# Linear attention and a sine layer on one core: the first chunk's loads, transposes and spare products in another order

## The chip, the core and the metric

The kernel runs on one core of a Trainium2 chip. The metric is the device time of one execution in microseconds, the median of several runs. A profile comes from one execution of its own, and its times are counted from the first instruction that the profiler saw (the span).

## What is computed

Linear attention with decay over B=4 sequences, H=8 heads, S=768 positions and D=64, in blocks of 64 positions, and behind it a layer with a sine:

```python
intra = np.einsum('bhic,bhjc->bhij', qb, kb) * Dmask[None]
intra = np.einsum('bhij,bhjd->bhid', intra, vb)
inter = np.einsum('bhid,bhde->bhie', qb * lam_pow[None], kv_state)
out[:, :, sl] = intra + inter
kv_state = lam_block * kv_state + np.einsum('bhsd,bhse->bhde', kb * rev_pow[None], vb)
...
h = x @ w_in                          # 3072 x 512 by 512 x 2048
s = np.sin(alpha * h)
g = h + s * s / (alpha + 1e-09)
return g @ w_out                      # 3072 x 2048 by 2048 x 512
```

`x` is the attention's output with the heads side by side.

## The kernel before, in words

The positions are cut into six chunks of 128 (`t` or `g`, 0 to 5); a chunk holds all four sequences (`b`), so 512 rows. While the layer runs for chunk g, the attention of chunk g+1 is woven in between. The order on every engine is the order of the program; nothing is rearranged by a scheduler. An engine waits only where it reads or reuses what another has not finished.

**Loads.** Two ways lead into the chip. SP's queue brings k and q of sequence 0 and q of sequence 1 of the first chunk as float32 (`raw`, L79 to L81) and then `alpha`. GpSimd's queue brings everything else and turns it to bfloat16 on the way: `load(t, nm, b0, b1)` (L100 to L104), `load_w_in0`, `load_w_in`, `load_w_out` (L88 to L98). For the first chunk its order is: index tables by `iota` (`pcol`, L110 to L117), the identity `iden`, the triangle `tri`, `pos_row`; then k of b=1, k of b=2 and 3, q of b=2 and 3 (L133, L134); then `idf`, both halves of v, five loads of `w_in`, and later two of `w_out`. GpSimd builds the list of packets of each of its loads itself and keeps at most eight loads outstanding: a further one waits for the eighth before it to land. The third and fourth part of `w_out` (L487, L488) stand behind chunk 1's k, q and v in that queue.

**The first chunk's attention** (L443 to L477). Its state is empty, so only the part inside the chunk is computed. ScalarE makes powers of lambda from `pcol` and `pos_row` (`powers`, `decay_tables`, `etab`); DVE casts raw k (L445), scales raw q (`scale_q`, L447) and makes the mask `C0` (L451) from `tri`. Then, per sequence b: TensorE transposes k and q into a bank of PSUM (`turns` for b=0 and 1, L221; `turns_pair` for b=2 and 3, L240, which does k of both sequences, then q of both); ScalarE, for one copy DVE, takes them to `QKT` (L231, L248, L250); `scores1` (L252) multiplies k and q, eight small products of two heads each, and DVE masks them (`STm`, L260); `outs` (L263) multiplies by v, and ScalarE (b=0 and 1, L276) or DVE (b=2 and 3, L278) takes the result to `xt`.

**Spare products.** `spin(n)` (L437) multiplies a tile of ones, `fill`, n times into a bank; nothing reads the result. It stands at the start (10), between the transposes of k and q of b=2 and 3 (6) and at the end (2).

**Order on the engines around the change.** TensorE: transposes b=0, b=1; scores b=0, b=1; the transpose of `alpha` (L461); k's late transposes (bank 1); six spare products; q's late transposes (bank 2, both sequences); scores b=2, b=3; outputs b=0 to 3; two spare products; the hidden layer. DVE: the copy of q's b=3, `alpha_sb` (L467) and its reciprocal (L468), four masks, two `xt`. ScalarE: the copies, the casts of outputs b=0 and 1, then the table for the sine and a warm-up of one element (L473, L474).

**The layer.** `hidden(g, f)` (L382) makes 128 of the 2048 hidden columns: four products (L386), the sine on ScalarE (L389), its square on ScalarE or DVE. `finish` (L397) puts the result into `gall` on DVE (L401). `project(g, m, part)` (L406) multiplies four of the sixteen blocks of `gall` by one of the four parts of `w_out` (L411); for chunk 0 the third parts come right behind the late transposes of chunk 1 (L537 to L545).

Of the kernel before, what the change touches and what calls it, by code (L numbers as in the profile page):

```python
# [9 lines left out]
ACTF = mybir.ActivationFunctionType  # L10
FP32 = mybir.dt.float32
BF16 = mybir.dt.bfloat16
# [3 lines left out]
def kernel(  # L16
# [11 lines left out]
    nc = tc.nc  # L28
    P = nc.NUM_PARTITIONS
# [4 lines left out]
    HP = H // 2  # L34
# [8 lines left out]
    consts = ctx.enter_context(tc.tile_pool(name="consts", bufs=1))  # L43
# [14 lines left out]
    def bank(nm, n, dtype=FP32):  # L58
        return psum.tile([P, 512 if dtype is FP32 else 1024], dtype, name=nm, tag=f"b{n}")

    HB = (0, 1, 2)
# [34 lines left out]
    def load_w_out(i):  # L96
        nc.gpsimd.dma_start(out=w_out_sb[i][:],
                            in_=moe_w_out[i * 512:(i + 1) * 512, :].rearrange("(f p) d -> p f d", p=P))  # L98

    def load(t, nm, b0, b1):  # L100
        dst, src = NAT[nm]
        nc.gpsimd.dma_start(  # L102
            out=dst[t][:, b0:b1, :, :].rearrange("p b h e -> p (b h) e"),
            in_=src[b0:b1, :, t * T:(t + 1) * T, :].rearrange("b h p e -> p (b h) e"))  # L104
# [2 lines left out]
    new_chunk(1)  # L107


    pcol = consts.tile([P, 5], FP32, name="pcol")  # L110
    for n, base, step in ((0, -1, -1), (1, 1, 1), (2, T - 1, -1)):
        nc.gpsimd.iota(out=pcol[:, n:n + 1], pattern=[[0, 1]], base=base, channel_multiplier=step,
# [5 lines left out]
    iden = consts.tile([P, P], BF16, name="iden")  # L118
# [7 lines left out]
    for n in (1, 2, 0):  # L126
# [3 lines left out]
    pos_row = consts.tile([P, T], FP32, name="pos_row")  # L130
    nc.gpsimd.iota(out=pos_row[:], pattern=[[1, T]], base=1, channel_multiplier=0,
                   allow_small_or_imprecise_dtypes=True)
    for nm, b0, b1 in (("k", 1, 2), ("k", 2, 4), ("q", 2, 4)):  # L133
        load(0, nm, b0, b1)  # L134
    idf = consts.tile([NFC, NFC], FP32, name="idf")
    make_identity(nc, idf[:])
    for nm, b0, b1 in (("v", 0, 2), ("v", 2, 4)):
# [6 lines left out]
    lnlam = consts.tile([P, H], FP32, name="lnlam")  # L144
# [41 lines left out]
    V, G, A = nc.vector, nc.gpsimd, nc.scalar  # L186
    xt = {}
    kdec = {}
    KT, QT, both = {}, {}, {}
    STm = {}  # L190
    def home(t, blk):
        return SBD[2 if blk else t % 2]
# [44 lines left out]
    def halves(hd):  # L237
        return slice(hd * D, (hd + 1) * D)

    def turns_pair(t, nm, b, bk, engines):  # L240
        ps = bank("T_ps", bk, BF16)[:].rearrange("p (u c i) -> p u c i", u=2, c=HP)
        src, n = (kn, 0) if nm == "k" else (qn, 1)
        for u in range(2):
            for hp in range(HP):
                nc.tensor.transpose(out=ps[:, u, hp, :], in_=src[t][:, b + u, 2 * hp:2 * hp + 2, :], identity=iden[:])
        for u, eng in enumerate(engines):
            if eng is nc.scalar:
                eng.copy(out=both[t][:, n, b + u, :, :], in_=ps[:, u])  # L248
            else:
                eng.tensor_copy(out=both[t][:, n, b + u, :, :], in_=ps[:, u])  # L250

    def scores1(t, b, ns):  # L252
        Fb = [bank("F0_ps", n)[:].rearrange("p (c i) -> p c i", c=HP) for n in ns]
        for hp in range(HP):
            for hd in range(2):
                nc.tensor.matmul(out=Fb[hd][:, hp, :], lhsT=KT[t][halves(hd), b, hp, :],  # L256
                                 rhs=QT[t][halves(hd), b, hp, :], start=True, stop=True)
        st = work.tile([P, 2, HP, T], BF16, name="STm")
        for hd in range(2):
            nc.vector.tensor_tensor(out=st[:, hd], in0=Fb[hd], in1=C0[:, hd], op=ALU.mult)  # L260
        STm[t, b] = st

    def outs(t, b, n, eng=None):  # L263
        O = bank("O_ps", n)[:].rearrange("p (c i) -> p c i", c=HP)
        if t:
            for hp in range(HP):
                nc.tensor.matmul(out=O[:, hp, :], lhsT=home(t, 0)[:, b, hp, :, :], rhs=QT[t][:, b, hp, :],
                                 start=(hp == 0), stop=False, skip_group_check=True)
        for hp in range(HP):
            for hd in range(2):  # L270
                nc.tensor.matmul(out=O[halves(hd), hp, :], lhsT=vn[t][:, b, 2 * hp + hd, :],
                                 rhs=STm[t, b][:, hd, hp, :], start=(t == 0 and hp == 0), stop=True,
                                 skip_group_check=True)
        x = xt[t][:, :, b * T:(b + 1) * T]
        if eng is nc.scalar:
            nc.scalar.copy(out=x, in_=O)  # L276
        else:
            nc.vector.tensor_tensor(out=x, in0=O, in1=Etab[:], op=ALU.mult)  # L278
# [155 lines left out]
            row = m * S + g * T  # L434
            nc.sync.dma_start(out=out[row:row + T, cols], in_=o_sb[:, 0:DM // 2])

    def spin(n, cols=512):  # L437
        ps = bank("hps", HB[0])
        for _ in range(n):
            nc.tensor.matmul(out=ps[:, 0:cols], lhsT=fill[:, 0:P], rhs=fill[:, 0:cols], start=True, stop=True)  # L440


    new_xt(0)  # L443
    spin(10)
    nc.vector.tensor_copy(out=kn[0][:, 0, :, :], in_=raw["k", 0][:])  # L445
    def scale_q(b):
# [14 lines left out]
    nc.tensor.transpose(out=a_ps[:, 0:NFC], in_=alpha_fp[:], identity=idf[:])  # L461
    alpha_sb = consts.tile([P, NFC], FP32, name="alpha_sb")
    r_sb = consts.tile([P, NFC], FP32, name="r_sb")
    turns_pair(0, "k", 2, 1, (A, A))
    spin(6)
    turns_pair(0, "q", 2, 2, (A, V))
    nc.vector.tensor_copy(out=alpha_sb[:], in_=a_ps[:, 0:NFC])  # L467
    nc.vector.reciprocal(out=r_sb[:], in_=alpha_sb[:])  # L468
    scores1(0, 2, (6, 7))
    scores1(0, 3, (4, 5))  # L470
    outs(0, 0, 0, A)
    outs(0, 1, 3, A)
    warm = consts.tile([P, 1], FP32, name="warm")  # L473
    nc.scalar.activation(out=warm[:], in_=lnlam[:, 0:1], func=ACTF.Sin)  # L474
    outs(0, 2, 1)
    outs(0, 3, 2)
    spin(2)  # L477
    load_w_out(0)
    load_w_out(1)
    decay_k(0, 0, 2)  # L480
# [156 lines left out]
```

## Time and profile before

| | us |
|---|---|
| three runs | 215.69, 217.07, 215.86 |
| median | 215.86 |
| the profiled execution | 215.78 |
| its span | 214.1 |
| TensorE matmul, busy in the span | 200.0 (93%) |
| ScalarE, busy | 140.6 (66%) |
| VectorE (DVE), busy | 139.0 (65%) |
| GpSimd (POOL), busy | 96.4 (45%) |
| GpSimd's load queue: 75968 packets, 13.24 MB | 84.5% of 16 engines' span |
| SP's load queue: 23648 packets, 11.28 MB | 26.9% of 16 engines' span |
| GpSimd: index tables, identity, triangle | 0.91 to 2.72 |
| GpSimd: issues of k b=1, then k b=2 and 3 | 2.66 to 4.88 |
| first product of the hidden layer | 20.40 |

Reading it: "busy" counts instructions of an engine from start to end; matmuls overlap each other, so 93% is not the array at its peak. A packet is one contiguous run of bytes. The views used are the page (its rows of tenths over 40 slices), the chain of waits (followed back from the last instruction: start, length, what ran), timelines of an engine, windows (length, then busy time and number of instructions of PE, weight loads, DVE, ACT and POOL, the granted clock, the transfer engines' share and GB/s), and the list of transfers with the time from issue to landing.

### The profile page before, as it was taken

What the parts mean: (1) busy time and instruction counts of PE and PEld (TensorE: products, weight loads), DVE (VectorE), ACT (ScalarE), POOL (GpSimd) and SP (SyncE); (2) the same over time, 40 slices, a digit from 0 to 9 for tenths busy, and PEclk for the clock granted to TensorE, in tenths of its full rate; (3) what the DMA queues carried; (4) which work ended last, traced back from release to release, by engine and by line L of the source; (5) the groups of instructions that cost most, each with busy time, mean ns of one, the idle gap of its engine ahead of it and who ended that gap; (6) DMA issues with size and microseconds to landing.
All of it is one profiled execution on the core that took longest, in us unless ns stands there. A gap on an engine that the chain in (4) does not pass through costs nothing.

```text
span 214.1 us, 4756 instructions
## 1 busy us (share of the span) xinstructions
PE 200.0 (93%) x1913; PEld 100.5 (47%) x1939; DVE 139.0 (65%) x251; ACT 140.6 (66%) x225; POOL 96.4 (45%) x111
## 2 busy tenths in 40 slices
PE   7486989999998999999999999999999999999993
PEld 2354444554444644446444456444446444444453
DVE  7637697865899966995757977648668544444000
ACT  5834997736766497667576765776765778888121
POOL 8999639795699995899001950003100000000000
PEclk9769999999999999999999999999999999999999
DMA  5999999999999999999999114911101001110212
GB/s 113 163 164 206 206 181 156 182 176 158 199 159 161 165 134 129 210 174 115 166 134 163 73 52 104 144 49 52 43 9 49 26 26 49 49 48 5 100 49 98
DMA packets 99782, 24.83 MB, mean 116 GB/s; under 512 B 91936, under 2 KB 96816, under 8 KB 99760
## 3 DMA queue, kind: packets, MB, share of 16 engines
q0 software_dynamic: 75968, 13.24, 84.5%
q1 hardware_dynamic: 23648, 11.28, 26.9%
q8 instruction: 15, 0.25, 0.5%
q14 instruction: 7, 0.06, 0.1%
q10 hardware_dynamic: 144, 0.00, 0.0%
HBM read 27.28 MB, written 6.29 MB: 157 GB/s over the span
## 4 chain that ended last, share of the span: by engine, by line
PE 78%; DVE 10%; ACT 5%; DMA 3%; issue 2%; POOL 1%; POOLq 0%; ACTq 0%
PE ops L411 35%; PE hps L386 32%; DVE gall L401 3%; DMA kn<-in_k_dram 3%; ACT s_sb L389 2%; DVE STm L260 2%; DVE S L297 2%; PE O_ps L352 2%; PE hps L429 2%; ACT s L392 2%; PE O_ps L360 1%; PE T_ps L227 1%; DVE s L400 1%; PE hps L440 1%; PE F_ps L256 1%
## 5 line engine op out<-in xcount | busy, mean ns | idle before, releaser
L401 DVE SCALAR_TENSOR_TENSOR gall<-s,r_sb,hps 128x512 bf16<-128x512 bf16 x96 | 70.9, 744 | 42.3 <-ACT s L392 42.0
L386 PE MATMUL hps<-xt,w_in 128*128 128x512 bf16 x377 | 95.6, 379 | 2.6 <-DVE gall L401 1.5
L389 ACT ACTIVATE s_sb<-hps,alpha_sb 128x512 bf16<-128x512 f32 x96 | 65.6, 687 | 42.7 <-PE hps L386 42.3
L411 PE MATMUL ops<-w_out,gall 128*128 128x512 bf16 x351 | 90.7, 379 | 0.9 <-issue 0.3
L386 PEld LDWEIGHTS <-w_in 128*128 128x128 bf16 x384 | 37.3, 98 | 46.6 <-issue 2.3
L392 ACT ACTIVATE s<-s_sb 128x512 bf16<-128x512 bf16 x87 | 54.9, 632 | 2.8
L411 PEld LDWEIGHTS <-gall 128*128 128x128 bf16 x368 | 34.6, 98 | 40.3 <-issue 0.6
L301 POOL CAST sbd<-S 64x512 bf16<-64x512 f32 x36 | 22.4, 623 | 45.4 <-DVE S L297 43.9
L204 POOL TENSOR_TENSOR kdec<-kn,R 128x1024 bf16<-128x1024 bf16 x12 | 22.6, 1901 | 0.4
L297 DVE SCALAR_TENSOR_TENSOR S<-S,L,KV_ps 128x128 f32<-128x128 f32 x64 | 17.3, 342 | 0.0
L102 POOL DMA_DIRECT2D vn<-in_v_dram x12 | 14.0, 1168 | 1.4 <-DMA w_in<-in_moe_w_in_dram 1.4
L420 ACT COPY o_sb<-ops 128x512 f32<-128x512 f32 x11 | 6.3, 577 | 12.2 <-PE ops L411 12.2
L102 POOL DMA_DIRECT2D kn<-in_k_dram x12 | 14.1, 1173 | 0.5 <-DMA kn<-in_k_dram 0.5
L102 POOL DMA_DIRECT2D qn<-in_q_dram x11 | 13.0, 1180 | 1.7 <-DMA qn<-in_q_dram 1.0
L260 DVE TENSOR_TENSOR STm<-F_ps,C 128x512 bf16<-128x512 f32 x16 | 10.1, 682 | 3.8 <-PE F_ps L256 3.7
L368 DVE TENSOR_TENSOR xt<-O_ps,Etab 128x512 bf16<-128x512 f32 x16 | 10.3, 685 | 2.5 <-PE O_ps L360 2.5
L418 DVE COPY o_sb<-ops 128x512 f32<-128x512 f32 x12 | 8.3, 692 | 4.9 <-PE ops L411 4.9
L341 DVE TENSOR_TENSOR STm<-F_ps,C 128x512 bf16<-128x512 f32 x16 | 10.3, 683 | 0.0
L440 PE MATMUL hps<-fill 128*128 128x512 bf16 x16 | 6.5, 565 | 1.7 <-DVE fill L121 1.5
L235 ACT COPY QKT<-T_ps 128x1024 bf16<-128x1024 bf16 x4 | 3.9, 1008 | 2.2 <-PE T_ps L227 2.2
L256 PE MATMUL F_ps<-QKT 64*128 64x128 bf16 x64 | 3.6, 239 | 1.7 <-ACT QKT L248 0.7
L400 DVE TENSOR_TENSOR s<-s_sb 128x512 bf16<-128x512 bf16 x9 | 5.1, 571 | 0.0
(71 smaller groups left out, 97.6 us busy)
## 6 DMA issues: line engine op xcount, KB each, us to landing
out_dram<-o_sb SPq DMA_DIRECT2D x23, 256.0 KB, 2.3
vn<-in_v_dram POOLq DMA_DIRECT2D x12, 256.0 KB, 15.1
kn<-in_k_dram POOLq DMA_DIRECT2D x11, 256.0 KB, 12.0
qn<-in_q_dram POOLq DMA_DIRECT2D x11, 256.0 KB, 14.0
w_out<-in_moe_w_out_dram POOLq DMA_DIRECT2D x4, 512.0 KB, 15.6
w_in<-in_moe_w_in_dram POOLq DMA_DIRECT2D x3, 512.0 KB, 12.2
raw_q<-in_q_dram SPq DMA_DIRECT2D x2, 256.0 KB, 5.2
w_in<-in_moe_w_in_dram POOLq DMA_DIRECT2D x2, 256.0 KB, 7.3
```

The lines of the kernel that those rows point to most:

```text
L102: nc.gpsimd.dma_start(out=dst[t][:, b0:b1, :, :].rearrange("p b h e -> p (b h) e"), in_=src[b0:b1, :, t * T:(t + 1) * T, :].rearrange("b h ...
L204: nc.gpsimd.tensor_tensor(out=kdec[t][:, b0:b1, :, :], in0=kn[t][:, b0:b1, :, :], in1=R[:].unsqueeze(1).unsqueeze(3).broadcast_to([P, b1 - ...
L260: nc.vector.tensor_tensor(out=st[:, hd], in0=Fb[hd], in1=C0[:, hd], op=ALU.mult)
L297: nc.vector.scalar_tensor_tensor(out=S[:, bs, hp, :], in0=old[:, bs, hp, :], scalar=decay[:, hp:hp + 1], in1=ps[:, :, hp, :], op0=ALU.mult ...
L301: nc.gpsimd.tensor_copy(out=dst[halves(hd), bs, :, hd, :], in_=S[halves(hd), bs, :, :])
L341: nc.vector.tensor_tensor(out=st[:, hd], in0=att["F"][pr, hd], in1=C64[:, hd].unsqueeze(1).broadcast_to([P, 2, HP, D]), op=ALU.mult)
L368: nc.vector.tensor_tensor(out=xview(t)[:, 2 * pr:2 * pr + 2, blk, :, :], in0=att["O"][pr, blk], in1=Eb, op=ALU.mult)
L386: nc.tensor.matmul(out=hps[:], lhsT=w[:, c, (f % 4) * P:(f % 4 + 1) * P], rhs=xt[g][:, c, :], start=(c == 0), stop=(c == NDC - 1))
L389: nc.scalar.activation(out=s_sb[:], in_=hps[:], func=ACTF.Sin, scale=alpha_sb[:, f:f + 1])
L392: nc.scalar.activation(out=s2[:], in_=s_sb[:], func=ACTF.Square)
L401: nc.vector.scalar_tensor_tensor(out=gall[g][:, f, :], in0=s2[:], scalar=r_sb[:, f:f + 1], in1=hps[:], op0=ALU.mult, op1=ALU.add)
L411: nc.tensor.matmul(out=ops[:], lhsT=gall[g][:, f, m * P:(m + 1) * P], rhs=w_out_sb[part][:, f % 4, :], start=(f == 0), stop=(f == NFC - 1))
```

## The change

Four things, all in the first chunk. GpSimd issues both loads of k ahead of its index tables, q's stays behind them. `turns_pair` takes two banks, one for each sequence; q's late transposes use banks 2 and 0, k's both bank 1 as before. The six spare products ahead of q's transposes are gone; instead one stands behind them, two behind the scores, two each behind the outputs of b=1 and b=2, and three instead of two at the end, each call in a bank that it names. On ScalarE the sine's table and the warm-up come ahead of the casts of outputs b=0 and 1; on DVE `alpha_sb` and the reciprocal come between the masks of b=2 and b=3.

```diff
     new_chunk(1)
+    load(0, "k", 1, 2)
+    load(0, "k", 2, 4)
     pcol = consts.tile([P, 5], FP32, name="pcol")
...
-    for nm, b0, b1 in (("k", 1, 2), ("k", 2, 4), ("q", 2, 4)):
-        load(0, nm, b0, b1)
+    load(0, "q", 2, 4)
     idf = consts.tile([NFC, NFC], FP32, name="idf")
...
     def turns_pair(t, nm, b, bk, engines):
-        ps = bank("T_ps", bk, BF16)[:].rearrange("p (u c i) -> p u c i", u=2, c=HP)
         src, n = (kn, 0) if nm == "k" else (qn, 1)
+        one = bank("T_ps", bk[0], BF16)[:].rearrange("p (u c i) -> p u c i", u=2, c=HP)
+        two = one if bk[0] == bk[1] else bank("T_ps", bk[1], BF16)[:].rearrange("p (u c i) -> p u c i", u=2, c=HP)
+        ps = (one[:, 0], two[:, 1])
...
-    def spin(n, cols=512):
-        ps = bank("hps", HB[0])
+    def spin(n, bk=0, cols=512):
+        ps = bank("hps", bk)
...
-    turns_pair(0, "k", 2, 1, (A, A))
-    spin(6)
-    turns_pair(0, "q", 2, 2, (A, V))
+    turns_pair(0, "k", 2, (1, 1), (A, A))
+    turns_pair(0, "q", 2, (2, 0), (A, V))
+    warm = consts.tile([P, 1], FP32, name="warm")
+    nc.scalar.activation(out=warm[:], in_=lnlam[:, 0:1], func=ACTF.Sin)
+    spin(1, 1)
+    scores1(0, 2, (6, 7))
     nc.vector.tensor_copy(out=alpha_sb[:], in_=a_ps[:, 0:NFC])
     nc.vector.reciprocal(out=r_sb[:], in_=alpha_sb[:])
-    scores1(0, 2, (6, 7))
     scores1(0, 3, (4, 5))
+    spin(2, 1)
     outs(0, 0, 0, A)
     outs(0, 1, 3, A)
-    warm = consts.tile([P, 1], FP32, name="warm")
-    nc.scalar.activation(out=warm[:], in_=lnlam[:, 0:1], func=ACTF.Sin)
+    spin(2, 1)
     outs(0, 2, 1)
+    spin(2, 2)
     outs(0, 3, 2)
-    spin(2)
+    spin(3, 4)
     load_w_out(0)
```

More of the change, by code (lines that the diff above doesn't have):

```diff
@@ L240, in turns_pair @@
     def turns_pair(t, nm, b, bk, engines):
-        ps = bank("T_ps", bk, BF16)[:].rearrange("p (u c i) -> p u c i", u=2, c=HP)
         src, n = (kn, 0) if nm == "k" else (qn, 1)
+        one = bank("T_ps", bk[0], BF16)[:].rearrange("p (u c i) -> p u c i", u=2, c=HP)
+        two = one if bk[0] == bk[1] else bank("T_ps", bk[1], BF16)[:].rearrange("p (u c i) -> p u c i", u=2, c=HP)
+        ps = (one[:, 0], two[:, 1])
         for u in range(2):
             for hp in range(HP):
-                nc.tensor.transpose(out=ps[:, u, hp, :], in_=src[t][:, b + u, 2 * hp:2 * hp + 2, :], identity=iden[:])
+                nc.tensor.transpose(out=ps[u][:, hp, :], in_=src[t][:, b + u, 2 * hp:2 * hp + 2, :], identity=iden[:])
         for u, eng in enumerate(engines):
             if eng is nc.scalar:
-                eng.copy(out=both[t][:, n, b + u, :, :], in_=ps[:, u])
+                eng.copy(out=both[t][:, n, b + u, :, :], in_=ps[u])
             else:
-                eng.tensor_copy(out=both[t][:, n, b + u, :, :], in_=ps[:, u])
+                eng.tensor_copy(out=both[t][:, n, b + u, :, :], in_=ps[u])
     def scores1(t, b, ns):
```

## The prediction

> **What bounds the kernel now.** I read the clock and transfer rows of the profile's second part first, then the chain of waits over the first 48 us, then the windows of the clock, the queues' packets and the transfers' landing times.
>
> ```profile
> PEclk9769999999999999999999999999999999999999
> DMA  5999999999999999999999114911101001110212
> ```
>
> Each digit is 5.35 us. The clock is low only in the first three slices. The transfer engines are 90% busy from the second slice to the 22nd, so whatever lands there lands when the queue gets to it.
>
> ```profile
> 2.66 5.59 DMA kn<-in_k_dram
> 8.29 1.05 PE T_ps L227 x8
> ...
> 12.50 2.33 PE hps L440 x5
> 14.83 0.46 PE T_ps L245 x8
> 15.29 0.02 issue
> 15.31 0.60 ACT QKT L248
> 15.91 0.02 issue
> 15.93 0.42 DVE QKT L250
> ...
> 16.72 2.33 DVE STm L260 x4
> 19.06 0.51 DVE xt L278
> 19.57 0.01 issue
> 19.57 0.69 DVE xt L278
> 20.26 0.14 issue
> 20.40 1.04 PE hps L386 x4
> ```
>
> The first chunk is one chain: k's load, the spare products (L440) between the transposes of k and q, two copies one after the other, four masks on DVE, the outputs to `xt`, and at 20.40 the first product of the hidden layer. From there PE is nearly always busy.
>
> ```profile
> 8.00:11.30 3.30, 2.39 (x26) 1.74 (x27) 2.03 (x5) 1.86 (x4) 3.30 (x5) 0.50 2.46 156
> 11.30:14.70 3.40, 3.18 (x15) 1.75 (x16) 1.10 (x2) 1.07 (x2) 3.08 (x5) 0.50 3.25 156
> 14.70:18.10 3.40, 2.29 (x49) 1.79 (x48) 2.13 (x6) 1.49 (x3) 3.39 (x4) 1.00 1.41 199
> ```
>
> After the length comes PE's busy time; the clock is third from the end. The clock fell at 7.9 and rose at 14.7, two steps of 3.4: 72% busy did not lift it, 94% did, and 67% kept it up.
>
> ```profile
> 28.92 0.75 POOL L97 DMA_DIRECT2D w_out<-in_moe_w_out_dram  x1 [1.38 <-DMA w_out<-in_moe_w_out_dram]
> w_out<-in_moe_w_out_dram POOLq DMA_DIRECT2D x1, 512.0 KB, 15.5
> 44.45 1.03 PE L411 MATMUL ops<-w_out,gall 128*128 128x512 bf16 x4
> ```
>
> The third part of `w_out`, issued at 28.92, lands 15.5 later, at 44.42. Its first product starts at 44.45. A front end that is ready earlier meets this load.
>
> **The change, part by part.** Times are those of the profiled execution: 215.78 us, a span of 214.1 and 1.68 around it; the median of the three runs is 215.86, 0.08 more.
>
> *GpSimd's order.* The two k issues took 2.22 us from 2.66; now they start at about 0.81, where SP and ScalarE start theirs. The index work (0.91 to 2.72) ends at about 4.9. Its readers: the exponentials from 5.39 (their columns ready by about 3.9), the transposes at 5.57 (`iden` at 4.5), `pos_row` at 6.56 (4.9), `C0` at 6.81 (`tri` at 4.7). The smallest slack is 1.1 us: nothing is lost, and without that cover at most 2.2 - 1.1 = 1.1 would be. GpSimd's sum up to q's issue is unchanged, so q, `idf`, v, `w_in` and `w_out` are issued as before (q at 4.86).
>
> What it costs lies on SP's queue: the raw loads of k0, q0 and q1 share the engines with k. In 4.0 to 4.5 the SP queue alone moved 559 packets. In 5.5 to 6.0, with GpSimd's queue alive, it moved 349 and the other 78; GpSimd's alone moved 614 to 621 in half a us from 7.5 on. Its packets begin about 2.3 us after the issue, so now at 3.1. At 846 falling to 730 SP packets per us, q0's 1024 end at 5.4 instead of 4.94 and q1's at 6.8 instead of 6.7; with the lag of 1.2 to 1.3 from last packet to landing, q0 lands at 6.6 (6.2 before) and q1 at 8.1. k's b=1 lands between 6.3 (equal turns) and 8.25 (no gain). Since `C0` stands between q0 and q1 on DVE, q1 is scaled 0.4 later, its transposes end at 9.7, the scores of b=0 start 0.4 later and those of b=1 at 10.35 instead of 10.49. From both sides: b=1 0.54 earlier if the raw loads lose nothing, 0.7 later at equal turns. I take the measured 349 to 78, the nearest row.
>
> The Trainium skill, DMA: Bandwidth & Descriptors, section "Queues, rings and completion order", has each engine take turns between its queues packet by packet. By that rule raw q0 would land at 7.5 and q1 at 9.4, and the scores of b=2 would start at 14.8 rather than at the 13.8 below. The packet counts of 5.5 to 6.0 are not equal turns.
>
> *No spare products ahead of q's late transposes.* Six were issued there, 2.55 us from 12.28 to 14.83. q's load lands at 4.86 + 7.0 = 11.9, so the transposes follow k's at once, from about 12.1, and at half clock take 1.03 (k's eight at L245) instead of 0.66: they end at 13.1 instead of 15.29, -2.2.
>
> *Two banks.* Before, DVE's copy (0.42) waited for ScalarE's (0.60). Now ScalarE copies k until 13.2 and q's b=2 until 13.75, with DVE's copy beside it. The one spare product needs k's bank, free at 13.2, and is done by 13.65. The scores of b=2 start at 13.8 instead of 15.95.
>
> *Masks, `alpha`, outputs.* Eight scores take 0.61 at half clock; DVE's first mask starts at 14.4. `alpha_sb` and the reciprocal (0.17 + 0.25) now stand between the two pairs of masks, where nothing hides them: 14.4 + 1.2 + 0.42 + 1.2 = 17.25 (19.05 before), and two `xt` (0.69 each) reach 18.6. PE must keep up: at full clock from 14.7, spare products of 0.215 and outputs of 0.4 bring O(0,3) to 17.8 and the first hidden product to **18.7**, -1.7. If the clock rises only at the next step, 18.1, spare products cost 0.43 and outputs about 0.6: O(0,3) ends at 19.15, `xt` at 19.85, the hidden product starts at **20.0**, -0.4. Window 11.3 to 14.7 would be some 90% busy, nearer to the row of 94% than to that of 72%, but two thirds of it are transposes.
>
> The Trainium skill, TensorE: Matmul & The Clock Gate, section "Part 4: PE-mode transpose", says that transposes do not count as busy in the same way. By it the term is -0.4 and not -1.7. The row of 72%, nearly all transposes and half-array scores, stayed at half clock and agrees, but does not separate kind from share.
>
> *Sine table.* Its load (1.28) and the warm-up (0.21) move from 18.29 to about 13.75, done at 15.2; ScalarE's first cast of an output comes at 15.7. Before they lay in idle time ahead of 21.46. Nothing both times; without that cover, a few tenths.
>
> *Later.* A front end shorter by 0.4 to 1.7 moves the whole first hidden stage, until a load is late. `w_in`'s second block lands at 20.06, used at 22.2 at the earliest; chunk 1's q lands at 35.0 against use at 36.30, so the largest gain loses 0.4 there. `w_out`'s third part, at 44.42 against 44.45, takes nearly all of any gain, if the queue's stream stays put. That it does: the engines do the same packets in the same order without a pause. Bounds: some 0.3 us of capacity unused between 2.5 and 3.3 could be filled (356 packets in 3.0 to 3.5 against 552), or 0.4 lost, because mixed queues moved 427 packets per half us against 559, over some 1.8 us more. I take 0. Behind it two PE waits of 0.20 and 0.16 may shrink: -0.2. Sum: 215.78 - 0.2 = **215.6**, own range 215.2 to 216.2.
>
> **The rivals.** *The gain passes.* If `w_out` lands with the shorter front end, 215.78 - 1.7 = 214.1, or 215.4 at the smaller term; with the full 2.2 of the transposes, 213.6. For it: no PE wait on `w_out` is named, so 44.45 need not be its limit. Against it: the landing time and the busy row.
>
> *The raw loads starve (slower).* If GpSimd's queue gets two packets of three once k is queued early, q0 lands at 8.95 and q1 at 11.8, the scores of b=2 start at 17.25 instead of 15.95, and with the 4.9 us from there (13.8 to 18.7, full clock) the hidden product starts at 22.1: +1.7, **217.5**, all of which passes on. It decides from where raw q1 lands after about 10.1 (8.1 before): 11.8 less the 1.7. Against it: 349 to 78 the other way. For it: GpSimd's queue overtook within 1 us (452 to 90 in 6.5 to 7.0).
>
> *The change doesn't do what it says:* k's early issue may bring k no sooner (8.25 above). That costs the forecast nothing, since q1's scaling is the later of the two.
>
> **How the numbers follow.** The load as the cap 0.53; the gain passes 0.27, of which 0.06 beyond 1%; starved raw loads 0.20, of which 0.07 beyond 1% (about the least that a measurement of this kernel tells from no change, 2.16 us here, read off the three runs' spread of 1.4). So faster 0.06, same 0.87, slower 0.07. The range for 8 in 10 reaches from 214.2, most of the passing gain, to 216.8, half of the starved case: 215.6 as the likeliest.
>
> **What would show it.** Right: raw q1 lands before 9; q's late transposes follow k's at once and end by 13.5; DVE's copy lies beside ScalarE's; the hidden stage begins between 18.7 and 20.0; and a new PE wait before the L414 products of `w_out`'s third part, with that load as releaser, near 44.4. The clock row between 14.7 and 18.1 tells which term holds. Wrong: no wait there and a `w_out` that lands sooner (gain passes), or raw loads after 10 and scores of b=2 after 15.95 (starved).

## The result, and the profile after

| | before | after |
|---|---|---|
| median of 20 runs of each, us | 215.88 | 217.00 |
| lowest to highest | 215.08 to 219.14 | 216.66 to 217.82 |
| the profiled execution, us (its span) | 215.78 (214.1) | 216.80 (215.1) |
| raw q1 landed / its scaling began | 7.5 / 7.95 | 10.07 / 10.10 |
| k's late transposes began | 11.31 | 13.44 |
| scores of b=2 began | 15.95 | 16.09 |
| first product of the hidden layer | 20.40 | 21.46 |

The ratio of after to before is 1.0054, with a 95% interval of 1.0038 to 1.0070: slower by half a per cent, clear of the scatter and inside 1%. So a difference of 1.1 can be told here, half of the 2.16 that the prediction took for about the least. The forecast was 215.6, within a range that ended at 216.8. Some executions take over 1.5% longer than the fastest of the same kernel, and the ratios leave them out. The changed kernel's lines are numbered three higher from the transposes on (L386 is now L389, L411 is L414).

The rows of tenths of the changed kernel:

```profile
PEclk9959999999999999999999999999999999999999
DMA  5999999999999999999999013911001011110212
```

The third slice holds a low clock, as before, and the transfer engines are 90% busy from the second slice to the 22nd, as before. No stage behind the first 21 us looks different. The chain of waits of the changed kernel (start, length, what ran):

```profile
1.94 8.13 DMA raw_q<-in_q_dram
...
10.10 0.70 DVE qn L450
...
13.44 0.98 PE T_ps L248 x8
...
14.44 1.08 ACT QKT L251 x2
...
16.16 0.58 PE F_ps L259 x8
16.74 1.28 DVE STm L263 x2
18.02 0.09 DVE alpha_sb L473
...
18.15 0.41 PE O_ps L274 x8
18.57 0.55 PE hps L443 x2
...
20.58 0.75 PE hps L443 x3
...
21.46 1.04 PE hps L389 x4
```

Before, the chain began with GpSimd's load of k (2.66, 5.59 long). Now it begins with SP's load of raw q, issued at 1.94 and 8.13 long. Its reader, DVE's scaling of q1, waits 1.91 for it and starts 2.15 later than before, when it waited for no load (first line before, second after; start, length, then in brackets the idle time ahead and what ended it):

```profile
7.95 0.68 DVE L447 TENSOR_TENSOR qn<-raw_q,Rq 128x512 bf16<-128x512 f32 x1
10.10 0.69 DVE L450 TENSOR_TENSOR qn<-raw_q,Rq 128x512 bf16<-128x512 f32 x1 [1.91 <-DMA raw_q<-in_q_dram]
```

K's late transposes start 2.13 later. From there the six spare products are gone and the two copies lie side by side, so that the scores of b=2 are only 0.14 late: the edits behind the loads gave back 2.0. Then the time from the scores of b=2 to the hidden layer is 5.37, where it was 4.45: another 0.92. The sum, 2.15 - 2.0 + 0.92, is 1.06 with rounding, and from 21.46 on every stage is late by about this (the next chunk's state products at 61.26 for 60.22, the last ones at 208.23 for 207.20).

The wait on the third part of `w_out` that the prediction named does not show:

```profile
28.60 0.75 POOL L97 DMA_DIRECT2D w_out<-in_moe_w_out_dram  x1 [1.38 <-DMA w_out<-in_moe_w_out_dram]
...
45.49 1.03 PE L414 MATMUL ops<-w_out,gall 128*128 128x512 bf16 x3
```

The load is issued at 28.60 and takes 15.5 as before: landed at 44.1, used at 45.49, without a wait. A kernel that is 1.06 late is not held by it.

The queues' packets say why raw q1 was late. These are the rows between 5.5 and 6.0, first of the kernel before, then of the changed one (queue, kind, packets, MB, share):

```profile
q1 hardware_dynamic: 349, 0.09, 110.2%
q0 software_dynamic: 78, 0.01, 30.2%
```

```profile
q0 software_dynamic: 617, 0.08, 245.5%
```

In these rows q0 names GpSimd's queue and q1 SP's; in the text q0 and q1 are the raw loads of sequences 0 and 1. In the changed kernel SP's queue has no row at all, though raw q1 had been issued at 1.94 (this took until 3.84, and from 3.88 to 4.73 SP issued the next load, `alpha`). Added up from the start, with three of the experiments below beside it (SP's packets / GpSimd's; the third number, in e11, is ScalarE's, 144 packets of which are its small load of lambda):

| up to | before | after | e7: half of k early | e11: raw q1 by ScalarE | e14: raw q in one load |
|---|---|---|---|---|---|
| 4.4 | 1570 / 0 | 1326 / 0 | 1372 / 0 | 785 / 0 / 364 | 564 / 0 |
| 5.0 | 2095 / 1 | 1887 / 138 | 1920 / 151 | 1080 / 0 / 602 | 982 / 0 |
| 5.4 | 2402 / 30 | 2073 / 402 | 2091 / 437 | 1132 / 0 / 944 | 1372 / 0 |
| 6.0 | 2826 / 120 | 2080 / 1135 | 2284 / 955 | 1540 / 13 / 1180 | 2048 / 3 |
| 6.4 | 3009 / 295 | 2087 / 1593 | 2576 / 1042 | 1910 / 86 / 1184 | 2475 / 31 |
| 7.0 | 3125 / 817 | 2175 / 2146 | 2937 / 1163 | 2077 / 592 / 1184 | 2880 / 185 |
| 8.0 | 3152 / 2014 | 2584 / 2593 | 3152 / 2089 | 2080 / 1817 / 1184 | 3104 / 1082 |

A load of one sequence is 1040 packets: 1024 of 64 values each and 16 more. In the changed kernel SP's queue stands at 2080 from about 5.5 to 6.2. That is exactly two loads: k0 and q0 are done, and q1 has not begun. Its first packet comes at 6.24. The table holds one thing more: by 4.4, with none of GpSimd's packets moved, SP's queue was already behind (1326 for 1570, and 1372 in e7). No run shows why.

### The profile page after: what moved, and what is told of

Read it like the earlier page. It is cut to its first block, busy times and chain, and to the rows that moved or that the text cites. A ratio compares the mean times of both kernels' runs of the same rounds, so it can differ in the third digit from the quotient of the medians.

```text
span 215.1 us, 4760 instructions
## 1 busy us (share of the span) xinstructions
PE 201.0 (93%) x1915; PEld 100.8 (47%) x1941; DVE 139.3 (65%) x251; ACT 140.2 (65%) x225; POOL 97.0 (45%) x111
## 4 chain that ended last, share of the span: by engine, by line
PE 79%; DVE 8%; ACT 5%; DMA 4%; issue 2%; SPq 0%; ACTq 0%
PE ops L414 35%; PE hps L389 33%; DMA raw_q<-in_q_dram 4%; DVE gall L404 3%; ACT s_sb L392 2%; DVE S L300 2%; DVE STm L263 2%; PE O_ps L355 2%; PE hps L432 2%; PE KV_ps L318 1%; ACT s L395 1%; PE O_ps L363 1%; PE F_ps L259 1%; PE hps L443 1%; PE T_ps L228 1%
## 5 line engine op out<-in xcount | busy, mean ns | idle before, releaser
L389 PE MATMUL hps<-xt,w_in 128*128 128x512 bf16 x377 | 95.6, 379 | 2.2 <-DVE gall L404 1.5
L414 PE MATMUL ops<-w_out,gall 128*128 128x512 bf16 x350 | 90.7, 379 | 1.0 <-issue 0.3
L389 PEld LDWEIGHTS <-w_in 128*128 128x128 bf16 x384 | 37.3, 98 | 46.4 <-issue 2.1
L414 PEld LDWEIGHTS <-gall 128*128 128x128 bf16 x368 | 34.6, 98 | 40.3 <-issue 0.6
L205 POOL TENSOR_TENSOR kdec<-kn,R 128x1024 bf16<-128x1024 bf16 x12 | 22.7, 1910 | 0.4
L443 PE MATMUL hps<-fill 128*128 128x512 bf16 x19 | 7.5, 525 | 1.8 <-DVE fill L123 1.5
L228 PE MATMUL T_ps<-iden,qn 128*128 128x128 bf16 x24 | 2.5, 234 | 3.8 <-DVE qn L450 3.8
## 6 DMA issues: line engine op xcount, KB each, us to landing
w_in<-in_moe_w_in_dram POOLq DMA_DIRECT2D x3, 512.0 KB, 10.9
```

What stands on the lines that cost most here:

```text
L205: nc.gpsimd.tensor_tensor(out=kdec[t][:, b0:b1, :, :], in0=kn[t][:, b0:b1, :, :], in1=R[:].unsqueeze(1).unsqueeze(3).broadcast_to([P, b1 - ...
L389: nc.tensor.matmul(out=hps[:], lhsT=w[:, c, (f % 4) * P:(f % 4 + 1) * P], rhs=xt[g][:, c, :], start=(c == 0), stop=(c == NDC - 1))
L414: nc.tensor.matmul(out=ops[:], lhsT=gall[g][:, f, m * P:(m + 1) * P], rhs=w_out_sb[part][:, f % 4, :], start=(f == 0), stop=(f == NFC - 1))
```

## The experiments

Medians are in us; each ratio is to the kernel before, run on the same chip beside it, with its 95% interval. A diff is against the changed kernel unless the text says otherwise.

**Which part costs the time (e1, e2).** e1 is the changed kernel with k's loads behind the index tables again; e2 is the kernel before with nothing but k's loads ahead of them.

```diff
 # e1
-    load(0, "k", 1, 2)
-    load(0, "k", 2, 4)
     pcol = consts.tile([P, 5], FP32, name="pcol")
...
+    load(0, "k", 1, 2)
+    load(0, "k", 2, 4)
     load(0, "q", 2, 4)
```

> The changed kernel with only GpSimd's order undone (index tables first, then k). Theory 'raw loads starve': raw q1 lands near 8.1 again instead of 10.06, the scores of b=2 start at 13.8 to 14.2 instead of 16.09, the first hidden product between 18.7 and 20.0 instead of 21.46. The time is then 215.6 if the third part of w_out (landing near 44.4) stops the gain, with a PE wait on that load, and 214.2 to 215.4 if it does not. Rival 'the missing spare products': the loss comes from the half clock behind the removed products, so the hidden product starts at 20.4 or later and the time is 216.2 to 217.

> The kernel before with only k's two loads issued ahead of the index tables. 'Raw loads starve': raw q1 lands near 10, the whole first chunk and the hidden layer behind it move by some 2 us (first hidden product near 22.4), 217.6 to 218. Rival 'the missing spare products', under which k early is harmless or a gain: 215.3 to 216.0.

e1: 215.48, ratio 0.9971 (0.9951 to 0.9992). e2: 218.89, ratio 1.0140 (1.0098 to 1.0182), some 0.9 more than expected. In e1 raw q1 is in time again (scaled at 7.95), the scores of b=2 start at 13.32 and the hidden layer at 18.69, 1.71 earlier than before. The end gains 0.3. This line of its timeline (start, length, engine and line, then the idle time ahead and what ended it) shows where most of the rest went:

```profile
44.40 1.02 PE L414 MATMUL ops<-w_out,gall 128*128 128x512 bf16 x3 [1.19 <-DMA w_out<-in_moe_w_out_dram]
```

TensorE is there early and waits 1.19 for `w_out`, after 0.28 for chunk 1's q at 35.03. In e2 the other half shows:

```profile
10.06 0.69 DVE L449 TENSOR_TENSOR qn<-raw_q,Rq 128x512 bf16<-128x512 f32 x1 [1.88 <-DMA raw_q<-in_q_dram]
```

The same late raw q1 with none of the other edits, and the hidden layer at 22.78, 2.38 late. So GpSimd's early issue is the whole loss, and the other edits together make the front end 1.7 shorter (in e1's profile; with the clock rising later it is 1.1 in e9's and 1.0 in e12's).

**Small terms in the stretch from the scores to the hidden layer (e3, e4).** e3 moves `alpha_sb` and the reciprocal ahead of the masks; e4 leaves out the six spare products between the scores of b=3 and the outputs of b=3.

```diff
 # e3
+    nc.vector.tensor_copy(out=alpha_sb[:], in_=a_ps[:, 0:NFC])
+    nc.vector.reciprocal(out=r_sb[:], in_=alpha_sb[:])
     scores1(0, 2, (6, 7))
-    nc.vector.tensor_copy(out=alpha_sb[:], in_=a_ps[:, 0:NFC])
-    nc.vector.reciprocal(out=r_sb[:], in_=alpha_sb[:])
 # e4
-    spin(2, 1)
     outs(0, 0, 0, A)
     outs(0, 1, 3, A)
-    spin(2, 1)
     outs(0, 2, 1)
-    spin(2, 2)
     outs(0, 3, 2)
```

> The changed kernel with alpha's copy and reciprocal ahead of the masks of b=2, as before the change. Theory 'late release of bank 3': the outputs of b=1 no longer wait for alpha's copy (18.02), the masks lose 0.42 between them, the first hidden product starts near 20.9 instead of 21.46, and the time is 216.4 to 216.6. Rival 'the spare products between the outputs set the pace': no gain, 216.9 to 217.1.

> The changed kernel without the six spare products between the scores and the outputs (one behind q's transposes and three at the end stay). 'Spare products on the path': outputs of b=3 wait for the mask (19.5) alone, the first hidden product starts near 21.0 instead of 21.46, 216.5 to 216.7. Rival 'they hold the clock': the clock stays or falls to half and the first hidden products run at 0.43 each, 217.5 to 218.5.

e3: 217.35, ratio 1.0058 (1.0034 to 1.0082), for 216.4 to 216.6 expected; the hidden layer at 21.26: 0.2 earlier, of which 0.09 was there at the scores already. `alpha` stands on the chain at 18.02 but is worth a tenth; its median is no better, six of its eight runs having the clock of 0.976. e4: 217.44, ratio 1.0062 (1.0040 to 1.0085). Its profiled execution is quicker (216.2, hidden layer at 20.87, 0.59 earlier), its median is not: six of its ten runs had a mean granted clock of 0.968 and took 217.1 to 218.1, a clock that none of the changed kernel's 20 runs had (0.976 to 1.0). So the spare products cost 0.6 on the chain; that they hold the clock is what these runs suggest.

**Is it `w_out` that caps the gain (e5, e6, e10, e9)?** In e5, e1's kernel, the third part of `w_out` is issued ahead of the second half of chunk 1's v; e6 does the same to the kernel before.

```diff
 # e5, against e1
-    for nm in "kqv":
-        load(1, nm, 2, 4)
+    load(1, "k", 2, 4)
+    load(1, "q", 2, 4)
     load_w_out(2)
+    load(1, "v", 2, 4)
```

> GpSimd's order undone as in e1, and the third part of w_out loaded one place earlier, ahead of chunk 1's second half of v. Theory 'the load of w_out takes the front end's gain': in e1 its first product waited 1.19 for the landing at 44.40. One load of 256 KB takes 1.7 of the queue, so the part lands near 42.8 and is wanted at 43.05: the wait goes, and the time is 214.1 to 214.5. Rival 'the gain is lost elsewhere as well' (chunk 1's v, q of the first half, DVE): 215.2 to 215.6.

> The kernel before with only the third part of w_out one place earlier. There it landed at 44.42 and was wanted at 44.45. Theory: it held nothing up, so no change, 215.6 to 216.0. Rival 'w_out already set the pace before': 214.3 to 215.3.

e6: 215.95, ratio 0.9990 (0.9961 to 1.0019), nothing, as a load on time should give. e5: 215.55, ratio 0.9983 (0.9952 to 1.0014), a miss, for 214.1 to 214.5 was expected: with the load moved up the time did not fall. Its profiled execution took 524.52 and shows nothing. So the same kernel ran again as e10.

> The kernel of e5 once more, for its profile. Theory: no wait on w_out, but a wait of 1 to 1.6 before the scores of chunk 2 (near 65 to 67) for q's transpose, which takes up the gain: 215.1 to 215.5. Rival: the wait on w_out is still there.

Five runs of e10 took 214.97 to 215.65, five 218.7 to 219.0; ratio 0.9976 (0.9942 to 1.0010). Its profile is of an execution of 218.92. The wait on `w_out` is gone there, the hidden layer starts at 18.75, and a wait of 3.90 stands at 68.97, for SP's transposed load of chunk 2's q (`QKT<-qn`, from one buffer of the chip to another). Its size holds for that execution alone; e7 below (215.81) shows the wait at 1.22. Chunk 3's loads go out on GpSimd's queue while that transposed load is under way, so e9 moves them three steps later.

```diff
 # e9, against e5
-            d[5 if g == 1 else 2] += [(new_chunk, t + 1), (pair_load, t + 1, 0)]
-            d[7 if g == 1 else 4] += [(pair_load, t + 1, 1)]
+            d[8 if g == 1 else 2] += [(new_chunk, t + 1), (pair_load, t + 1, 0)]
+            d[8 if g == 1 else 4] += [(pair_load, t + 1, 1)]
```

> As e5 (GpSimd's order undone, third part of w_out one place earlier), and both halves of chunk 3's loads issued in slot 8 of stage 1 instead of slots 5 and 7, so behind SP's four transposes of chunk 2. Theory 'GpSimd's queue starves SP's here too': in e7 the second q transpose (issued 60.05) landed 7.3 later and the scores of chunk 2 waited 1.22 for it; with the loads moved it lands in some 3.3 like the ones before it, there is no such wait, and the front end's 1.7 shows: 214.1 to 214.6. Rival 'another bound comes next': 215.0 to 215.6.

e9: 215.00, ratio 0.9955 (0.9931 to 0.9979), faster than both kernels, though not by what was expected (214.1 to 214.6), and no run of the twelve above 215.66. Against e5 and e10 the gain is not clear of the scatter, for the intervals overlap. Neither wait is there, and the scores of chunk 2 (L337) start at 65.04, 1.2 earlier than in the kernel before. From its list of waits between 80 and 90:

```profile
PE KV_ps L318 <- DMA vn<-in_v_dram: 0.6, 1, 0.6
```

Chunk 3's v, issued later, now comes 0.6 late and takes back half. The end is 0.42 earlier than before. A front end 1.1 shorter in that profile (19.29) meets three loads one behind the other: `w_out`, chunk 2's q, chunk 3's v.

**Half of k early (e7).** e1 with only k of b=1 ahead of the index tables.

```diff
 # e7, against e1
+    load(0, "k", 1, 2)
     pcol = consts.tile([P, 5], FP32, name="pcol")
...
-    load(0, "k", 1, 2)
     load(0, "k", 2, 4)
```

> The changed kernel with only k of b=1 (1024 packets) ahead of the index tables and k of b=2 and 3 (2048 packets) behind them. 'Raw loads starve' by what is queued on GpSimd's side: raw q1 lands between 8.1 and 10.06, near 8.8; the first hidden product near 19.6 to 20.4; 215.3 to 216.2. Rival 'the mere start of GpSimd's queue does it': raw q1 again near 10, 216.8 to 217.2.

216.01, ratio 0.9998 (0.9979 to 1.0017). Raw q1 lands at 8.36 and is scaled at 8.39, the hidden layer starts at 19.95. Further on stands the wait that takes the gain of 0.45 away:

```profile
67.44 0.45 PE L337 MATMUL F_ps<-QKT 64*64 64x64 bf16 x32 [1.22 <-DMA QKT<-qn]
```

In the table, GpSimd's queue goes through its one load of 1040 and stops near 6.2; SP's has q1 under way by then (its first packet at 5.35). One early load of 1040 makes q1's scaling 0.44 late, the two of the change (1040 and 2064) 2.15.

**The two banks and the sine table (e8, e12).** Both are e1 with one edit undone: q's late transposes in one bank, or the table and its warm-up back behind the casts.

```diff
 # e8, against e1
-    turns_pair(0, "q", 2, (2, 0), (A, V))
+    turns_pair(0, "q", 2, (2, 2), (A, V))
 # e12, against e1
-    warm = consts.tile([P, 1], FP32, name="warm")
-    nc.scalar.activation(out=warm[:], in_=lnlam[:, 0:1], func=ACTF.Sin)
     spin(1, 1)
...
     outs(0, 1, 3, A)
+    warm = consts.tile([P, 1], FP32, name="warm")
+    nc.scalar.activation(out=warm[:], in_=lnlam[:, 0:1], func=ACTF.Sin)
```

> As e1, but q's late transposes in one bank again. Theory: DVE's copy waits for ScalarE's once more, the scores of b=2 and the first hidden product come 0.3 to 0.5 later than in e1 (18.69), and the wait on w_out takes it up: 215.4 to 215.7, no change against e1. Rival: the two banks are what shortened the front end, first hidden product 19.5 or later.

> As e1, with the sine's table and warm-up behind the casts of outputs b=0 and 1 again. Theory: they lay in idle time at both places, so the first hidden product stays within 0.2 of 18.69 and the time within 0.3 of e1. Rival: the casts come earlier or the first sine later by up to 1.3.

e8: 215.56, ratio 0.9961 (0.9933 to 0.9990). e12: 215.55, ratio 0.9973 (0.9948 to 0.9998). Neither moves the time against e1, as the cap on `w_out` would have it: both still wait about 0.7 for it. DVE's copy of q's b=3 in e8 and then in e1:

```profile
13.74 0.42 DVE L253 COPY QKT<-T_ps 128x512 bf16<-128x512 bf16 x1 [1.61 <-ACT QKT L251]
```

```profile
12.95 0.42 DVE L253 COPY QKT<-T_ps 128x512 bf16<-128x512 bf16 x1 [1.01 <-PE T_ps L248]
```

In one bank the copy waits for ScalarE's, in two for the transposes alone. What the bank is worth at the hidden layer can't be read from this pair: it starts at 19.39 in e8, at 18.69 in e1, but the clock rose at 16.1 in the one and at 14.3 in the other, and e9 and e12, with two banks and a late clock, start at 19.29 and 19.45. In e12 the table's load lies in idle time ahead of the first sine, as before; the 0.76 by which its hidden layer is later than e1's can't be split from the clock either.

**How the queues take turns (e11, e13, e14, e15).** e11 has ScalarE's queue carry raw q1.

```diff
 # e11
-        nc.sync.dma_start(out=raw[nm, int(b)][:], in_=NAT[nm][1][int(b), :, 0:T, :].rearrange("h p e -> p h e"))
+        (nc.scalar if b == "1" else nc.sync).dma_start(out=raw[nm, int(b)][:], in_=NAT[nm][1][int(b), :, 0:T, :].rearrange("h p e -> p h e"))
```

> The changed kernel (k early) with raw q1 issued by ScalarE at 1.24 instead of by SP as its third load at 2.5. Theory: an earlier place in a queue of its own lets it through before GpSimd's queue flows; raw q1 lands before 8.5, the first hidden product near 19 to 19.8: 215.3 to 216.0. Rival 'every such queue starves once GpSimd's flows': raw q1 again near 10, 216.7 to 217.4.

216.53, ratio 1.0037 (1.0008 to 1.0066): a miss for both theories. Raw q1 lands at 6.8, but raw q0 at 7.91 (6.2 before). GpSimd's queue isn't the cause, since it had moved 86 packets by 6.4. ScalarE's load went ahead of SP's second one, whose count stands between 1080 and 1132 from 5.0 to 5.4. DVE's timeline in e11:

```profile
8.01 0.69 DVE L450 TENSOR_TENSOR qn<-raw_q,Rq 128x512 bf16<-128x512 f32 x1 [2.11 <-DMA raw_q<-in_q_dram]
8.62 1.22 DVE L454 TENSOR_TENSOR C<-tri,NE 128x1024 f32<-128x1024 f32 x1
9.76 0.69 DVE L450 TENSOR_TENSOR qn<-raw_q,Rq 128x512 bf16<-128x512 f32 x1
```

`C0` stands behind the late q0, and q1, long landed, behind `C0`. Three more runs tell the loads from the order on DVE, and whole loads in turn from a queue that goes first.

```diff
 # e13
-    load(0, "k", 2, 4)
+    load(0, "k", 2, 3)
+    load(0, "k", 3, 4)
 # e14 (C0 goes ahead of both scalings on DVE as well)
...
+    raw_q = rawp.tile([P, 2 * H, D], FP32, name="raw_q")
+    nc.sync.dma_start(out=raw_q[:], in_=q[0:2, :, 0:T, :].rearrange("b h p e -> p (b h) e"))
+    raw["q", 0], raw["q", 1] = raw_q[:, 0:H, :], raw_q[:, H:2 * H, :]
 # e15, against e11 (DVE: C0, q1, q0)
-    scale_q(0)
     nc.vector.tensor_tensor(out=C0[:], in0=tri[:].unsqueeze(1).unsqueeze(1).broadcast_to([P, 2, HP, T]),
                             in1=NE[:].unsqueeze(3).broadcast_to([P, 2, HP, T]), op=ALU.mult)
+    scale_q(1)
+    scale_q(0)
...
     turns(0, 0, 4, (A, A))
-    scale_q(1)
```

> The changed kernel, with k's load of b=2 and 3 as two loads of 1040 packets each (1024 rows and 16 more) in place of one of 2080. Whole loads in turn (an engine goes through a load that it has begun, then turns to the other queue): GpSimd's queue stands near 1040 packets while SP's goes through q1, as with half of k early; raw q1 lands at 8.4 to 8.9 (10.06 in the changed kernel), the hidden stage begins at 19.9 to 20.5, 215.8 to 216.2 us. GpSimd's queue first (it takes the engines as long as it has packets): no change, raw q1 at 10 or later, the hidden stage at 21.4 to 21.8, 217.0 us or a little more, since the third issue takes 1 us more of GpSimd.

> The changed kernel, with raw q of b=0 and 1 as one load on SP's queue in place of two, and C0 ahead of both scalings on DVE. Whole loads in turn: SP's queue no longer stops at 2080 packets, but goes through to about 3100 by 7.0, raw q lands near 8.2, q1 is scaled at 8.9 to 9.1 (10.10 in the changed kernel), the hidden stage begins at 20.2 to 20.5, 215.7 to 216.0 us. GpSimd's queue first: SP's queue stops in the middle of the load at 5.4, raw q lands at 10 or later, both scalings behind it, the hidden stage at 22 or later, 217.5 us or more.

> Raw q1 issued by ScalarE as before, and on DVE C0, then q1's scaling, then q0's (it was q0, C0, q1). Whole loads in turn: what the earlier run lost was DVE's order, since both raw loads had gone through by 7.0; q1 is scaled at 6.9, q0 at 8.0, the transposes of b=1 follow those of b=0, the scores of b=2 start at 13.8 to 14.3 (15.74 there), the hidden stage at 19.3 to 19.9, 215.5 to 215.9 us, held then by w_out's third part. GpSimd's queue first (the loads are what is lost): raw q1 or q0 again lands at 10, the hidden stage begins at 21 or later, 216.5 us.

e13: 216.91, ratio 1.0044 (1.0026 to 1.0062). SP's queue stands at 2080 again, and GpSimd's doesn't stop at 1040 but runs on to 1344 by 6.2; raw q1 lands at 9.86. That is about what "GpSimd's queue first" expected. e14: 215.96, ratio 0.9986 (0.9956 to 1.0016). Its packets from the start to 6.8:

```profile
q1 hardware_dynamic: 2777, 0.71, 47.7%
q0 software_dynamic: 93, 0.01, 2.7%
```

SP's queue does not stop: 3104 by 8.0, and GpSimd's, issued at 1.33 (1.34 in the changed kernel), has moved 93 by 6.8. Its first packets came at 5.9 and not at 4.4, so k0's end, near 5.0, was no hand-over. That is what "whole loads" expected, and with k's issue left early it wins back 1.0 of the 1.1 lost (the place of `C0` is not what was won: in the changed kernel it was done at 8.20, ahead of raw q1). The median says so; the trace is weaker, for the profiled execution, 217.15, is its only run above 216.1. In it every queue began late (ScalarE's first packet at 2.35 for 1.84, SP's at 2.94 for 2.38, from the same issue times), so part of GpSimd's late start is not the order of the loads, and raw q landed at 8.6. e15: 216.13, ratio 1.0013 (0.9995 to 1.0031). Both raw loads have gone through by 7.0, the hidden layer starts at 20.37, 0.75 earlier than e11's and 0.5 later than expected: q1's scaling waits for `C0` until 7.65, both sequences come at once, and ScalarE's four copies queue up (scores of b=2 at 15.00).

So neither of the two rules holds alone. Shown: where GpSimd's first packet found q1 already begun (before, 4.99 and 4.98), q1 went through with few of GpSimd's beside it, and so did q in e14; where it came while q0 was under way, SP's queue stood still behind q0, in the changed kernel, e2 and e13 at exactly 2080. Once q1 has begun among GpSimd's packets it doesn't go through undivided: in the changed kernel it needs 3.2 from its first packet to its last. Open: when GpSimd's queue hands back. It did so at 1040 where it had nothing more (e7), and near 1300 to 1400 where it had (e13, the changed kernel). The counts are of all 16 engines together, so what one engine did is not shown; nor is it shown that q1's packets stood ready at 5.45, though SP had gone on to the next issue by then.

## Why the prediction was wrong

**The step that failed** is the size of the raw loads' delay. It took "the measured 349 to 78, the nearest row" as the rate at which SP's queue and GpSimd's share the engines, and raw q1 landed at 10.07, not 8.1. (The "8.1 before" beside the rival was a slip as well: the load took 5.6 from 1.94 and landed at 7.5, some 0.6 behind its last packets, for a lag of 1.2 to 1.3 taken.) The row was no rate. The table shows what it was in the kernel before: GpSimd's first packets came as raw q1 began, and got through only as it ended; as I read it, the half us from 5.5 to 6.0 holds engines that had finished q1 beside those that hadn't. The other figure of that sum, 846 a us (423 in 4.5 to 5.0), was no share either: GpSimd's queue moved one packet there. With k issued early, GpSimd's packets came while q0 was under way, and q1 was still waiting: the hand-over one load sooner puts 1419 packets ahead of q1's first. That q0's last packet came at 5.45, as forecast (5.4), was partly luck: GpSimd's first packet came at 4.45, not at 3.1, and SP's queue was slow before that. A row of a mixture in which one side is ending can't be carried to another moment; the packets counted up from the start, which I did not lay beside the loads' sizes, would have shown the hand-over.

By the Trainium skill, DMA: Bandwidth & Descriptors, section "Queues, rings and completion order", an engine drains a whole packet of up to 64 descriptors from one ring before it turns to the next. I had read this as turns of single rows, which gave 9.4. The measurements agree with it in that turns are long. From GpSimd's first packet to q1's first it was 1.8 in the changed kernel (4.45 to 6.24), 1.7 in e13 and 0.9 in e7; at the 614 packets per half us of GpSimd's queue alone, spread evenly over 16 engines, an engine takes 130 to 140 in such a time, and 70 in e7's (an estimate). So two turns of 64, with the last packet of q0 (65 an engine) between them, would fit the stop as well as a rule by loads. The run e14 fits less: from 5.90 to 7.0 SP's queue moved 936 packets and GpSimd's 185, without a stop in the middle of the 129 that are q's on each engine.

**The rival of starved loads, given 0.20, is what happened**, with its point of decision (raw q1 after about 10.1) just about met at 10.07 and its time 217.5 against 217.0. Its mechanism, two packets of three for GpSimd's queue, was not right, so the nearness of its time is luck: SP's queue got nothing for 0.8 us, then little, and about half of the packets from 7.0 to 9.0; q0, said to land at 8.95, was scaled at 6.37.

**The front end without the early issue was right in its parts.** The prediction's 18.7 for the hidden layer is 18.69 in e1, but two misses cancel there: the scores of b=2 start at 13.32 for 13.8, and the stretch behind them is longer by the 0.47 below. Its "spare products gone, -2.2" and "one copy beside the other" show in the changed kernel too (q's transposes from 14.20, directly behind k's; DVE's copy at 15.30 beside ScalarE's from 14.44).

**The cap by `w_out` was right as far as it went, and could not show in the changed kernel.** In e1 the wait stands where the prediction put it, 44.40, the chain of waits runs through that load (28.91, 15.45 long), and the median is 215.48 for a forecast of 215.6. So "the gain passes" is refuted by e1, for the kernel without the early issue. But `w_out` is not the only cap: with it moved up (e5, e10) the time stayed, since the next late loads take the gain, as e9 shows in part.

**The clock's term.** By the Trainium skill, TensorE: Matmul & The Clock Gate, section "Part 4: PE-mode transpose", transposes do not count as busy in the same way, which would have made the gain 0.4. In e1 a window of 3.3 us, 93% busy, 1.78 of its 3.06 busy us transposes, was followed by the clock's rise at 14.3, and the gain was 1.71. In e9 and e12 the clock rose only at 15.5 and 16.2, and the hidden layer started at 19.29 and 19.45. So the two terms of the prediction, 18.7 and 20.0, hold the measured ones between them; which one comes differs from execution to execution. The traces bear the page out in part: in steps of 3.4 at half clock, 2.80 busy us with 0.13 of transposes lifted the clock (e12, 12.8 to 16.2), 2.79 with 1.50 did not (e9, 8.7 to 12.1), nor did 3.01 with 1.89 (e14, 12.1 to 15.6). So busy time alone does not decide, and transposes seem to count for less; that they count for something, e1 shows, with 3.18 and 1.78 (10.9 to 14.3).

**From the scores to the hidden layer, a term mis-sized by 0.47.** The prediction had 4.9, the changed kernel and e1 have 5.37. DVE's masks and `xt` were to set the pace; the chain of the changed kernel shows TensorE's own spare products, 0.55 a pair for the 0.43 taken, and three at the end. e4 puts them at 0.59, e3 `alpha` at about 0.1.

**Smaller steps.** The index tables were hidden, as said: ScalarE's exponential that reads `pcol` starts at 5.49 for 5.39. GpSimd's first issue was to start at 0.81 and started at 1.34, and q's issue, said to stay at 4.86, came at 5.63; neither is on the chain. The sine table is worth nothing, as said (e12). The stream of later loads kept its times (`w_out` at 44.1 for 44.42).

## What to carry to other kernels

When a load is issued earlier, ask which load of another queue is under way at the moment when its packets arrive, and which is still waiting: here the one still waiting stood for 0.8 us, while one already begun went through (before). Two small loads on the queue that matters offered the other queue a gap between them, and one load of both sizes closed it (e14, by its median). A front end made shorter is worth only the way to the next late load, so look up the landing times of all loads behind it before counting the gain (1.71 became 0.3).

## What the runs showed of the hardware

The queues do not share the engines in any fixed ratio: 559 packets per half us for SP's queue alone, 614 to 621 for GpSimd's alone, and only 413 to 457 for both together between 7.0 and 9.0 in the changed kernel. SP's transposed load of chunk 2's second half of q, issued at about 60 beside GpSimd's loads of chunk 3, lands 6.6 later in the kernel before and 7.3 in e7, and 4.4 later in e9, where those loads come three steps later.

GpSimd's first load issue began at 1.34, half a us later than those of SP at 0.81, with nothing ahead of it on the engine but four small fills that ended at 0.5; its own work was partly slower (the select for `idf` 1.25 for 0.51, `pos_row` 0.46 for 0.25), but the early loads are not shown to be the cause: with the same ones the select took 0.19 in e3, e11 and e14, and `pos_row` 0.25 in e11 and e14.

The mean granted clock of an execution comes in steps, and the time with it: of the runs of the kernel before beside e9 to e12, those at 0.992 took 215.1 to 215.9, at 0.984 215.9 to 216.7, at 0.976 217.1 to 217.5, at 0.968 219.1 to 219.4. The loss of the changed kernel is not this: its runs at 0.983 to 1.0 took 216.66 to 217.05. A mean of 1.0 does not say that the clock never fell: in e3's profile, at 1.0, k's eight late transposes take 1.03, as at half clock before.
